# Cross terms of a complex product formed on VectorE instead of from copies made by ScalarE

## The chip, the cores and the metric

The kernel runs on one core of a Trainium2 chip. The metric is the device time of one execution in microseconds (us). In the tables and rows, PE is TensorE (PEld its weight loads), DVE is VectorE, ACT is ScalarE, POOL is GpSimd and SP is the queue that issues most DMAs. [...]

## The reference, cut to what matters

The output is a sum of the input, a long convolution per channel and a feed-forward network, both of the layer-normalized input. L = 2048 rows, D = 576 channels, 128 states, FF = 4608.

```
xn  = layernorm(x)
K   = Re sum_n C[d,n] exp(dt A[d,n] l) dt B[d,n]         # a kernel of 2048 taps per channel
y   = irfft(rfft(pad(xn)) * rfft(pad(K)))[:L] + xn*Dskip
out = x + y + silu(xn @ w1) @ w2
```

The product of the two spectra is a complex multiplication, element by element: with U = ur + i ui and K = kr + i ki, its real part is ur kr - ui ki and its imaginary part is ui kr + ur ki. The terms with ki are called cross terms here. They are what the change is about.

## The kernel before, in words

TensorE works through the feed-forward network from end to end: 18 chunks (`blocks`, two halves of the sequence times nine chunks of FF, each for two blocks of 512 rows), with matmuls called `ph` (x times w1, 128x512) and `po` (hidden times w2, 128x288). Each float32 operand is split into a high and a low part (`xh`, `xl`, `w1h`, `w1l`, `gh`, `gl`), and three partial products stand for one. For each `ph`, ACT applies silu (`gf`, L351) and rounds it (`gh`, L352) and DVE forms the low part (`gl`, L354); ACT also makes `w1h` and `w2h` and DVE `w1l` and `w2l` of each new weight; DVE adds each `po` to `acc` (L373).

The convolution is woven between these (`weave`): a generator `side` yields at marks of progress. Its stages are: normalization, the taps of the convolution kernel (`natural`, `kgen`, up to about 655 us), the spectral stage (`spectral`, about 655 to 975 us) and the last transform with the stores (`tail`).

The spectral stage handles 16 pairs of frequencies, p = 0 to 15. For each p it transforms a tile of the kernel (`kw`, kind 0), a tile of the input (`u`, kind 1) and, after the product, transforms back (`ysw`, kind 2). The matmuls (`pf`, L815) of all three are packed into 27 *visits* of TensorE, counted 0 to 26 here; a visit fills four PSUM banks, of which there is one set (`psb`, bufs=1), so that the next visit can start only when all copies out of the last have ended. ACT copies out `ka` and `ut` (L833) and `e` (L825); DVE forms the two halves of `yo` from `e` and PSUM (L827), `yo` is written to DRAM. Visit 5 holds the end of input 3, visit 16 the start of the back transform of product 8, visit 25 first the end of input 15 and then, as a second piece with feed-forward matmuls between, the back transform of product 14.

The *product* of p (`products`, L835 to L852) starts when its `ut` is complete. Real parts lie on partitions 0 to 63, imaginary parts on 64 to 127, and g counts two groups of 576 columns. ACT makes `kb` from `ka`, with the halves swapped and one negated (L840, L841), and then overwrites the imaginary half of `ka` by the real one (L842). DVE multiplies `kb` by the swapped `ut` (L845, L846), `ut` by `ka` (L847) and adds (L848). Four DMAs on SP (L851) then reorder the partitions into `ysw`, which a visit two or three places later reads. There is one `kb` for both groups, so ACT can't fill it for p+1 before the last addition of p. On DVE, the product is followed by `halves` (L799, L801), which prepares a later `kw`.

The order on each engine comes from a scheduler of the tile framework: it plays the program through with a cost model of its own and emits whatever it finds ready, by priority. If the instructions of one part change, others around it move too.

Of the kernel before, what the change touches and what calls it, by code (L numbers as in the profile page):

```python
# [11 lines left out]
F32 = mybir.dt.float32  # L12
# [3 lines left out]
ALU = mybir.AluOpType  # L16
# [3 lines left out]
P = 128  # L20
L = 2048
D = 576
# [21 lines left out]
def kernel(  # L44
# [22 lines left out]
    nc = tc.nc  # L67
# [22 lines left out]
    cst = ctx.enter_context(tc.tile_pool(name="cst", bufs=1))  # L90
    ident = cst.tile([P, P], F32, name="ident")
    f1 = vt = None
    s4 = None
# [16 lines left out]
    pss = psb = ps3 = None  # L110
# [39 lines left out]
    pins = {}  # L150
# [306 lines left out]
                    for kt in {"d3": (0, 1), "u1": (2, 3), "u2": (4,)}.get(step, ()):  # L457
                        split_xt(b, kt)

    kl = yp = pa = tail_at = None  # L460
    kf = {}

    def steps():

        NT, NP = 6, 96
        dt = cst.tile([NP, NT], F32, name="dt")
        nc.sync.dma_start(dt, log_dt.rearrange("(p t) -> p t", t=NT))

        e1 = cst.tile([NP, NT], F32, name="e1")
        e2 = cst.tile([NP, NT], F32, name="e2")  # L470
        ec = float(np.float32(math.e))
        nc.vector.memset(e1, ec)
        with behind(pins["xt7"]):
            nc.vector.tensor_scalar(e2, dt, 1.0 - math.log(ec), 1.0, op0=ALU.mult, op1=ALU.add)
        with behind(pins["sd"]):
            nc.gpsimd.tensor_tensor(e1, e1, dt, op=ALU.pow)
        nc.vector.tensor_mul(dt, e1, e2)
        dh = cst.tile([NP, NT], F32, name="dh")
        nc.vector.tensor_scalar(dh, dt, 0.5, None, op0=ALU.mult)
        return dt, dh  # L480

# [272 lines left out]
    def spectral():  # L754

        NP = 16
# [78 lines left out]
        def products(p):  # L835

            ut, ka = uts.pop(p), kas.pop(p)
            kb = kl.tile([P, 2, D], F32, tag="kb", name="kb", bufs=1)
            for g in range(2):
                nc.scalar.mul(kb[:64, g], ka[64:, g], -1.0)  # L840
                nc.scalar.copy(kb[64:, g], ka[64:, g])  # L841
                nc.scalar.copy(ka[64:, g], ka[:64, g])  # L842
            yield
            for g in range(2):
                nc.vector.tensor_mul(kb[:64, g], ut[64:, g], kb[:64, g])  # L845
                nc.vector.tensor_mul(kb[64:, g], ut[:64, g], kb[64:, g])  # L846
                nc.vector.tensor_mul(ut[:, g], ut[:, g], ka[:, g])  # L847
                pins["turned"] = nc.vector.tensor_add(ut[:, g], ut[:, g], kb[:, g]).ins  # L848
            ys[p] = kl.tile([P, 2, D], F32, tag="ys", name="ysw")
            for o in (0, 2, 1, 3):  # L850
                nc.sync.dma_start(ys[p][32 * o:32 * o + 32], ut[32 * (0, 2, 1, 3)[o]:32 * (0, 2, 1, 3)[o] + 32])  # L851
            yield  # L852
# [117 lines left out]
        return t + min(max(t - turn, 0) * lost / (0.5 - turn - lost), lost)  # L970

    def side():
        nonlocal s4, kl, yp, pa, tail_at, f1, vt, pss, psb, ps3
        marks = (0.13, 0.601, 0.876)
        tail_at = (0.91, 0.934, 0.967, 0.0072)
        with tc.tile_pool(name="kf", bufs=1) as kfp, tc.tile_pool(name="pss", bufs=3, space=PSUM) as pss, tc.tile_pool(name="ps3", bufs=1, space=PSUM) as ps3:
            for n in ("f", "phi"):
                kf[n] = kfp.tile([P, D], F32, name=n + "T")
            f1 = kfp.tile([P, P], F32, name="f1")
            vt = kfp.tile([P, 69], F32, name="vt")  # L980
            with tc.tile_pool(name="par", bufs=1) as par:
                with tc.tile_pool(name="pa", bufs=4) as pa:

                    zero = pa.tile([P, 512], BF16, name="zero", bufs=1)
                    nc.vector.memset(zero, 0.0)
                    pz = ps1.tile([P, 512], F32, tag="ps1", name="pz")

                    def idle(n):
                        for _ in range(n):
                            nc.tensor.matmul(pz, zero[:, :P], zero, start=True, stop=True)  # L990

                    idle(12)
                    p01, p23 = phase0(pa, (0, 1), idle), phase0(pa, (2, 3))
                    next(p01)
                    yield 0
                    next(p23)
                    yield 0
# [12 lines left out]
                    yield 0  # L1010
                with tc.tile_pool(name="nat", bufs=1) as nat, tc.tile_pool(name="pb", bufs=1) as pb:
                    nt = natural(nat, par)
                    def late(j):

                        xs = load_x(j, pb, "xj", (nc.sync,))
                        yield
                        with behind(pins["xn" if j == 8 else "gl"]):
                            normed(pb, (j, j + 1), xs)
                        yield

                    tiles = chain.from_iterable(late(j) for j in range(8, NJ, 2))
                    for at, todo in ((0.0, nt), (0.0, tiles), (0.004, tiles), (0.005, tiles), (gate_of(0), nt), (0.026, tiles), (0.028, tiles), (0.036, tiles), (0.038, tiles), (gate_of(1), nt), (0.06, tiles), (gate_of(2), nt), (0.09, nt)):
                        yield at
                        with behind(pins["gl"] if at else pins["xt7"] if todo is nt else None):
                            next(todo, None)
            with behind(pins["sd"]):
                nc.gpsimd.dma_start(f1, cf1)
            nc.sync.dma_start(vt, cv)
            with tc.tile_pool(name="up", bufs=1) as up:
                sp = spread(up)  # L1030
                for n, at in enumerate(kgen()):
                    yield paced(at, marks)
                    for off in (0.4, 0.8):
                        if n > 1 and n % 2 == (1 if off < 1 else 0):
                            yield paced(at + off % 1 / 36, marks)
                            next(sp, None)
                for _ in sp:
                    pass
        s4p = ctx.enter_context(tc.tile_pool(name="s4p", bufs=1))
        s4 = s4p.tile([P, 2, 32], F32, name="s4")  # L1040
        nc.gpsimd.dma_start(s4, cs4)

        ps3 = None
# [106 lines left out]
```

## Time and profile before

| what | us |
|---|---|
| median of 3 runs (lowest, highest) | 1095.03 (1094.64, 1095.66) |
| the profiled execution | 1095.03 |
| its span on the core | 1093.2 |
| PE busy | 1082.7 |
| DVE busy | 891.6 |
| ACT busy | 631.4 |
| POOL busy | 138.4 |

The span runs from the first to the last instruction of the program; 1.8 us of the execution lie around it. An interval in which TensorE is busy is not all spent at its peak, since the records of successive matmuls overlap. A row of the list of groups gives a line, the engine, the operation, tiles, shape and count, then the time the group kept its engine busy, the mean duration of one in ns, and the idle time just before them with what ended it. A row of the timeline gives start, duration and instruction, and in brackets the engine's idle time before it. A row of the windows gives a stretch, its length, the busy time of PE, PEld, DVE, ACT and POOL with their counts, the granted clock of TensorE (1.00 is full speed), the DMA share and GB/s.

### The profile page before, as it was taken

The numbers are of one execution on the slowest core, as the hardware profiler recorded it, in microseconds if no ns is written. First come the engines' busy times: TensorE is split into PE (matmuls) and PEld (weight loads), VectorE is DVE, ScalarE is ACT, GpSimd is POOL, SyncE is SP. The second block draws the span as 40 slices with busy tenths as digits, with TensorE's granted clock in tenths as the row PEclk, the third lists the DMA queues.
The fourth block names the chain that finished last, engine by engine and source line by source line (L and its number), as shares of the span: only waits on it lengthen the run. The fifth ranks groups of instructions, "written<-read, shape, count | busy, mean of one in ns | idle before, by whom it ended". The sixth has DMA issues, their size and how long they took to land.

```text
span 1093.2 us, 24683 instructions
## 1 busy us (share of the span) xinstructions
PE 1082.7 (99%) x10127; PEld 947.1 (87%) x10127; DVE 891.6 (82%) x1463; ACT 631.4 (58%) x998; POOL 138.4 (13%) x241
## 2 busy tenths in 40 slices
PE   9999999999999999999999999999999999999998
PEld 7999998998998999889999898878787787888886
DVE  7799899999999999999999954677987878553443
ACT  4574455767676777676676653746666665532210
POOL 1101000000000000010000004323242331000111
PEclk9999999999999999999999999999999999999999
DMA  9745521342525243427643257567676875337953
GB/s 263 215 125 157 141 68 40 94 112 66 130 71 134 71 110 95 112 89 193 211 132 102 73 113 189 147 180 221 196 218 175 232 195 160 101 101 205 244 161 87
DMA packets 175424, 156.58 MB, mean 143 GB/s; under 512 B 113312, under 2 KB 144800, under 8 KB 175184
## 3 DMA queue, kind: packets, MB, share of 16 engines
q1 hardware_dynamic: 159616, 103.21, 36.9%
q0 software_dynamic: 14944, 50.94, 15.5%
q8 instruction: 79, 1.29, 0.5%
q10 hardware_dynamic: 752, 0.85, 0.3%
q14 instruction: 33, 0.27, 0.1%
HBM read 101.00 MB, written 44.61 MB: 133 GB/s over the span
## 4 chain that ended last, share of the span: by engine, by line
PE 81%; DVE 10%; ACT 3%; DMA 3%; issue 2%; SPq 0%; POOL 0%; DVEq 0%; ACTq 0%
PE po L369 35%; PE ph L343 30%; PE pf L815 4%; PE ph L345 3%; PE ph L344 3%; PE kp L736 2%; PE z L663 1%; DVE acc L373 1%; PE py L950 1%; DMA acc<-in_A_u_dram 1%; DVE gl L354 1%; DVE th L649 1%; DMA ysw<-ut 1%; DVE w1l L305 1%; PE pu L171 1%
## 5 line engine op out<-in xcount | busy, mean ns | idle before, releaser
L369 PE MATMUL po<-w2h,gh 128*128 128x288 f32 x1152 | 338.8, 297 | 0.7 <-DVE acc L373 0.6
L369 PE MATMUL po<-w2l,gh 128*128 128x288 f32 x1152 | 338.5, 296 | 0.0
L369 PE MATMUL po<-w2h,gl 128*128 128x288 f32 x1152 | 336.0, 296 | 0.0
L369 PEld LDWEIGHTS po<-w2h,gh 128*128 128x128 f32 x1152 | 215.2, 188 | 15.2 <-issue 3.8
L369 PEld LDWEIGHTS po<-w2l,gh 128*128 128x128 f32 x1152 | 215.7, 188 | 8.4 <-issue 2.3
L369 PEld LDWEIGHTS po<-w2h,gl 128*128 128x128 f32 x1152 | 215.0, 188 | 5.3 <-issue 4.3
L351 ACT ACTIVATE gf<-ph 128x512 f32<-128x512 f32 (+1 forms) x146 | 85.7, 588 | 176.9 <-PE ph L345 157.6
L373 DVE TENSOR_TENSOR acc<-po,acc 128x288 f32<-128x288 f32 x288 | 126.7, 454 | 69.7 <-PE po L369 68.6
L343 PE MATMUL ph<-xh,w1l 128*128 128x512 f32 (+1 forms) x584 | 159.4, 387 | 0.0
L343 PE MATMUL ph<-xh,w1h 128*128 128x512 f32 (+1 forms) x584 | 158.9, 388 | 0.3 <-ACT w1h L303 0.3
L343 PE MATMUL ph<-xl,w1h 128*128 128x512 f32 (+1 forms) x584 | 158.3, 386 | 0.0
L354 DVE TENSOR_TENSOR gl<-gf,gh 128x512 fp32r<-128x512 f32 (+1 forms) x148 | 98.8, 673 | 44.6 <-ACT gh L352 43.6
L343 PEld LDWEIGHTS ph<-xh,w1l 128*128 128x128 f32 x584 | 106.9, 188 | 21.4 <-issue 1.4
L343 PEld LDWEIGHTS ph<-xl,w1h 128*128 128x128 f32 x584 | 107.2, 188 | 20.6
L343 PEld LDWEIGHTS ph<-xh,w1h 128*128 128x128 f32 x584 | 104.0, 188 | 17.4 <-ACT w1h L303 0.6
L352 ACT CAST gh<-gf 128x512 fp32r<-128x512 f32 (+1 forms) x148 | 89.1, 611 | 41.0 <-PE po L369 38.3
L174 POOL DMA_DIRECT2D d1u<-u x32 | 17.4, 543 | 478.8 <-ACT u L173 470.6
L693 ACT ACTIVATE c<-th,magic 128x1040 f32<-128x1040 f32 x36 | 42.0, 1167 | 39.7 <-DVE C L716 32.0
L695 ACT ACTIVATE c<-th 128x1040 f32<-128x1040 f32 x36 | 38.6, 1073 | 45.4 <-DVE th L694 45.3
L305 DVE TENSOR_TENSOR w1l<-w1r,w1h 128x640 fp32r<-128x640 f32 x72 | 57.0, 820 | 0.3 <-ACT w1h L303 0.3
L345 PE MATMUL ph<-x,w1l 128*128 128x512 f32 (+1 forms) x146 | 56.7, 389 | 0.0
L344 PE MATMUL ph<-x,w1h 128*128 128x512 f32 (+1 forms) x146 | 56.3, 386 | 0.0
(191 smaller groups left out, 1656.4 us busy)
## 6 DMA issues: line engine op xcount, KB each, us to landing
w2r<-in_B_w_dram SPq DMA_DIRECT2D x72, 288.0 KB, 3.7
w1r<-in_B_w_dram SPq DMA_DIRECT2D x35, 512.0 KB, 4.0
d1u<-u POOLq DMA_DIRECT2D x32, 288.0 KB, 2.8
d1k<-stage SPq DMA_DIRECT2D x36, 256.0 KB, 4.9
u<-d1u POOLq DMA_DIRECT2D x16, 576.0 KB, 5.3
kw<-d1k POOLq DMA_DIRECT2D x16, 576.0 KB, 5.2
ysw<-ut SPq DMA_DIRECT2D x64, 144.0 KB, 3.6
d<-yo POOLq DMA_DIRECT2D x32, 288.0 KB, 4.0
```

Of the source, the lines that this page charges most:

```text
L305: pins["w1l"] = nc.vector.tensor_sub(l1, src, h1).ins
L343: nc.tensor.matmul(ph, w[:, kt, :], v[:, kt, a:e], start=n + kt == 0, stop=False)
L344: nc.tensor.matmul(ph, h1[:, 4, :], x4[:, a:e], start=False, stop=False)
L345: pins["pe"] = nc.tensor.matmul(ph, l1[:, 4, :], x4[:, a:e], start=False, stop=True).ins
L351: nc.scalar.activation(gf, ph, AF.Silu)
L352: pins["gh"] = nc.scalar.copy(gh, gf).ins
L354: pins["gl"] = nc.vector.tensor_sub(gl, gf, gh).ins
L369: pins["pe"] = nc.tensor.matmul(po[:, :HD], G[blk, t][g][:, js], W2[half, c, t][w][:, hs], start=n == 0, stop=n == 3 * FT - 1).ins
L373: nc.vector.tensor_add(acc[j][:, hs], po[:, :HD], acc[j][:, hs])
L693: nc.scalar.activation(c65, th, AF.Identity, bias=magic)
L695: nc.scalar.activation(c65, th, AF.Abs)
L815: last = nc.tensor.matmul(banks[os, g, b, at:at + n], mats[p, kind // 2][gs, os], src[:, c:c + n], start=True, stop=True, tile_position=(6 ...
```

## The change

ACT's two copies into `kb` go. DVE forms the cross terms itself, from `ut` and the still unchanged imaginary half of `ka`: one as a plain multiplication, the other, with its sign, as a scalar_tensor_tensor with the constant -1.0. ACT's copy of the real half over the imaginary one (now L842 of the changed kernel) has to wait until both have read it, and DVE's next multiplication waits for that copy. `kb` is now one group large, with three buffers. All four steps of a product stand in one loop over g. To make room in SBUF, the small tiles of `steps` move to a pool that is released earlier, and the constant tables `f1` and `s4` no longer have tiles of their own: they are loaded over `ident`, so their DMAs on POOL have to wait until the last reader of what stood there before.

```
     def steps():
...
-        dt = cst.tile([NP, NT], F32, name="dt")
+        dt = kfp.tile([NP, NT], F32, name="dt")
...
         def products(p):
 
             ut, ka = uts.pop(p), kas.pop(p)
-            kb = kl.tile([P, 2, D], F32, tag="kb", name="kb", bufs=1)
             for g in range(2):
-                nc.scalar.mul(kb[:64, g], ka[64:, g], -1.0)
-                nc.scalar.copy(kb[64:, g], ka[64:, g])
+                kb = kl.tile([P, D], F32, tag="kb", name="kb", bufs=3)
+                nc.vector.tensor_mul(kb[64:], ut[:64, g], ka[64:, g])
+                nc.vector.scalar_tensor_tensor(kb[:64], ut[64:, g], -1.0, ka[64:, g], op0=ALU.mult, op1=ALU.mult)
                 nc.scalar.copy(ka[64:, g], ka[:64, g])
+                nc.vector.tensor_mul(ut[:, g], ut[:, g], ka[:, g])
+                pins["turned"] = nc.vector.tensor_add(ut[:, g], ut[:, g], kb).ins
             yield
-            for g in range(2):
-                nc.vector.tensor_mul(kb[:64, g], ut[64:, g], kb[:64, g])
-                nc.vector.tensor_mul(kb[64:, g], ut[:64, g], kb[64:, g])
-                nc.vector.tensor_mul(ut[:, g], ut[:, g], ka[:, g])
-                pins["turned"] = nc.vector.tensor_add(ut[:, g], ut[:, g], kb[:, g]).ins
             ys[p] = kl.tile([P, 2, D], F32, tag="ys", name="ysw")
...
-            f1 = kfp.tile([P, P], F32, name="f1")
+            f1 = ident
...
-        s4p = ctx.enter_context(tc.tile_pool(name="s4p", bufs=1))
-        s4 = s4p.tile([P, 2, 32], F32, name="s4")
+        s4 = ident[:, :64].rearrange("p (q k) -> p q k", q=2)
         nc.gpsimd.dma_start(s4, cs4)
```

The scheduler emits the same instructions as before on PE, in another order from the gap between visits 4 and 5 on; up to there the order on all engines but for the two loads is the same. ACT has 64 instructions fewer, DVE as many as before. Three places show what moves. In these rows a line number is that of the kernel the row is from.

On ACT between visits 7 and 9, before: the copies for product 5 (L840, L841) stand ahead of the rounding of two new weights (`w1h`, L303).

```order
L352 CAST gh<-gf 128x512
L840 ACTIVATE kb<-ka 64x576
L841 COPY kb<-ka 64x576
L840 ACTIVATE kb<-ka 64x576
L841 COPY kb<-ka 64x576
L303 CAST w1h<-w1r 128x640 x2
L326 CAST w2h<-w2r 128x576
L351 ACTIVATE gf<-ph 128x512
L842 COPY ka<-ka 64x576
L825 COPY e<-pf 128x448
```

The same place with the change:

```order
L842 COPY ka<-ka 64x576 x2
L352 CAST gh<-gf 128x512 x2
L351 ACTIVATE gf<-ph 128x512 x2
L352 CAST gh<-gf 128x512
L303 CAST w1h<-w1r 128x640 x2
L326 CAST w2h<-w2r 128x576
L352 CAST gh<-gf 128x512
L825 COPY e<-pf 128x448
```

No `kb` copy stands between `gh` and `w1h` any more; the two copies L842 of product 4 come ahead of all of it.

On ACT after visit 21, before: `e` of 128 columns and `e` of 448 columns are copies out of this visit, `ut` of 64 columns is the last of them.

```order
L825 COPY e<-pf 128x128
L840 ACTIVATE kb<-ka 64x576
L841 COPY kb<-ka 64x576
L840 ACTIVATE kb<-ka 64x576
L841 COPY kb<-ka 64x576
L842 COPY ka<-ka 64x576
L825 COPY e<-pf 128x448
L842 COPY ka<-ka 64x576
L351 ACTIVATE gf<-ph 128x512
L352 CAST gh<-gf 128x512
L833 COPY ut<-pf 128x2x64
```

With the change:

```order
L833 COPY ka<-pf 128x2x384
L825 COPY e<-pf 128x128
L825 COPY e<-pf 128x448
L351 ACTIVATE gf<-ph 128x512 x2
L833 COPY ut<-pf 128x2x64
```

Six of the eight instructions between the first `e` and `ut` that don't copy out of the visit are gone from between them.

On DVE, product 14, before: `gl` and two `w1l` of the feed-forward stand inside the product.

```order
L845 TENSOR_TENSOR kb<-ut,kb 64x576
L846 TENSOR_TENSOR kb<-ut,kb 64x576
L845 TENSOR_TENSOR kb<-ut,kb 64x576
L846 TENSOR_TENSOR kb<-ut,kb 64x576
L373 TENSOR_TENSOR acc_6374<-po,acc_6374 128x288
L827 TENSOR_TENSOR yo<-e,pf 128x256 x2
L847 TENSOR_TENSOR ut<-ut,ka 128x576 x2
L354 TENSOR_TENSOR gl<-gf,gh 128x512
L305 TENSOR_TENSOR w1l<-w1r,w1h 128x640
L848 TENSOR_TENSOR ut<-ut,kb 128x576
L305 TENSOR_TENSOR w1l<-w1r,w1h 128x640
L848 TENSOR_TENSOR ut<-ut,kb 128x576
```

With the change:

```order
L354 TENSOR_TENSOR gl<-gf,gh 128x512 x2
L305 TENSOR_TENSOR w1l<-w1r,w1h 128x640 x2
L840 TENSOR_TENSOR kb<-ut,ka 64x576
L373 TENSOR_TENSOR acc_6373<-po,acc_6373 128x288
L841 SCALAR_TENSOR_TENSOR kb<-ut,ka 64x576
L840 TENSOR_TENSOR kb<-ut,ka 64x576
L841 SCALAR_TENSOR_TENSOR kb<-ut,ka 64x576
L373 TENSOR_TENSOR acc_6373<-po,acc_6373 128x288
L827 TENSOR_TENSOR yo<-e,pf 128x256 x2
L843 TENSOR_TENSOR ut<-ut,ka 128x576 x2
L844 TENSOR_TENSOR ut<-ut,kb 128x576 x2
```

The feed-forward's instructions stand ahead of the product now. Product 8 moves alike: two `w1l` and a `w2l` that stood inside it come ahead of it.

On PE, the feed-forward matmuls that stand between two visits change in number. Where the prediction uses them, these are their counts, read from the order of both kernels:

| between | before | with the change |
|---|---|---|
| visits 4 and 5 | 21 po, 3 ph | 22 po, 3 ph |
| visits 5 and 6 | 26 po, 27 ph | 27 po, 18 ph |
| visits 6 and 7 | 38 po, 15 ph | 33 po, 12 ph |
| visits 14 and 16, both gaps | 56 po, 38 ph | 56 po, 33 ph |
| visits 21 and 22 | 33 po, 24 ph | 42 po, 30 ph |
| visits 24 and 25 | 30 po, 22 ph | 33 po, 22 ph |
| the two pieces of visit 25 | 22 po, 11 ph | 19 po |

More of the change, by code (lines that the diff above doesn't have):

```diff
@@ L458, in ffn @@
                         split_xt(b, kt)
-    kl = yp = pa = tail_at = None
+    kl = kfp = yp = pa = tail_at = None
     kf = {}
@@ L465, in steps @@
         NT, NP = 6, 96
-        dt = cst.tile([NP, NT], F32, name="dt")
+        dt = kfp.tile([NP, NT], F32, name="dt")
         nc.sync.dma_start(dt, log_dt.rearrange("(p t) -> p t", t=NT))
-        e1 = cst.tile([NP, NT], F32, name="e1")
-        e2 = cst.tile([NP, NT], F32, name="e2")
+        e1 = kfp.tile([NP, NT], F32, name="e1")
+        e2 = kfp.tile([NP, NT], F32, name="e2")
         ec = float(np.float32(math.e))
@@ L477, in steps @@
         nc.vector.tensor_mul(dt, e1, e2)
-        dh = cst.tile([NP, NT], F32, name="dh")
+        dh = kfp.tile([NP, NT], F32, name="dh")
         nc.vector.tensor_scalar(dh, dt, 0.5, None, op0=ALU.mult)
@@ L972, in side @@
     def side():
-        nonlocal s4, kl, yp, pa, tail_at, f1, vt, pss, psb, ps3
+        nonlocal s4, kl, kfp, yp, pa, tail_at, f1, vt, pss, psb, ps3
         marks = (0.13, 0.601, 0.876)
```

## The prediction

> **What bounds the kernel now.** I read the page first, then the windows, the waits of TensorE, the groups, and last the timeline around each wait.
>
> ```profile
> span 1093.2 us, 24683 instructions
> PE 1082.7 (99%) x10127; PEld 947.1 (87%) x10127; DVE 891.6 (82%) x1463; ACT 631.4 (58%) x998; POOL 138.4 (13%) x241
> 100.00:600.00 500.00, 499.56 (x5004) 454.54 (x5003) 479.15 (x728) 330.34 (x499) 22.17 (x38) 1.00 0.41 109
> 655.00:955.00 300.00, 297.39 (x2915) 243.43 (x2914) 223.32 (x372) 175.64 (x298) 89.24 (x155) 1.00 0.67 184
> ```
>
> TensorE is the bound: 1082.7 of 1093.2 us, at the full granted clock of 1.00. The change adds and removes nothing on TensorE. In the spectral stage, which it touches (second window), TensorE is idle for 300 - 297.4 = 2.6 us; that is what a better order of the other engines can win there. ACT, which loses work, is busy 176 of 300 us, so its load is no bound; only its order can matter. Who made TensorE wait in this stage is in the waits (us in total, times, longest):
>
> ```profile
> PE pf L815 <- ACT ut L833: 1.0, 1, 1.0
> PE pf L815 <- DMA ysw<-ut: 0.6, 1, 0.6
> PE pf L815 <- issue: 0.5, 1, 0.5
> PE ph L343 <- ACT w1h L303: 0.3, 1, 0.3
> ```
>
> Four waits, 2.5 us. The forecast is a ledger: which of the four go, and which new ones come where visits move closer to what feeds them.
>
> **The change, part by part.** First the work itself.
>
> ```profile
> L840 ACT ACTIVATE kb<-ka 64x576 f32<-64x576 f32 x32 | 21.9, 684 | 28.9 <-DVE ut L848 28.4
> L841 ACT COPY kb<-ka 64x576 f32<-64x576 f32 x32 | 21.5, 671 | 0.4
> L842 ACT COPY ka<-ka 64x576 f32<-64x576 f32 x32 | 20.9, 672 | 0.6
> L846 DVE TENSOR_TENSOR kb<-ut,kb 64x576 f32<-64x576 f32 x32 | 24.2, 756 | 1.0
> L847 DVE TENSOR_TENSOR ut<-ut,ka 128x576 f32<-128x576 f32 x32 | 23.5, 752 | 0.1
> L554 DVE SCALAR_TENSOR_TENSOR e<-ex,r 128x576 f32<-128x576 f32 x4 | 3.0, 750 | 0.0
> L801 DVE SCALAR_TENSOR_TENSOR kw<-kw,cwt 128x576 f32<-128x576 f32 x32 | 26.2, 817 | 0.7
> ```
>
> ACT loses 32 x 684 + 32 x 671 ns = 43.4 us, and the 28.4 us that it stood at the head of `kb`, waiting for the product before. DVE replaces 32 multiplications of 756 ns by 32 scalar_tensor_tensor. Their size has no row; the nearest is L554, also with a constant, 750 ns, so I take no difference. With the 817 ns of L801, whose scalar is a tile, it would be 32 x 61 ns = 2.0 us in 300 us, of which DVE is idle 77. Nothing of this is on TensorE's path by itself: cost 0, covered by the feed-forward matmuls.
>
> To turn rows of the order into time I need the pace of the matmuls, from the chain of waits:
>
> ```profile
> 1066.15 2.74 PE ph L343 x12
> 1069.35 4.78 PE po L369 x36
> ```
>
> One ph is 2.74/12 = 0.228 us, one po 4.78/36 = 0.133 us.
>
> *Wait for w1h (after visit 8).* Start, duration, idle time in brackets:
>
> ```profile
> 771.89 0.68 ACT L840 ACTIVATE kb<-ka 64x576 f32<-64x576 f32 x1
> 773.99 0.67 ACT L841 COPY kb<-ka 64x576 f32<-64x576 f32 x1
> 774.68 1.36 ACT L303 CAST w1h<-w1r 128x640 fp32r<-128x640 f32 x2
> 775.46 1.20 PE L343 MATMUL ph<-xh,w1h 128*128 128x512 f32 x4 [0.33 <-ACT w1h L303]
> ```
>
> Four kb copies, 2.8 us, run right ahead of the rounding for which TensorE waits. They are gone, so the wait goes: -0.33 (between -0.33 and 0, if the two gf ahead of it now come late).
>
> *Wait of visit 22 for visit 21's copies.*
>
> ```profile
> 907.28 0.69 ACT L840 ACTIVATE kb<-ka 64x576 f32<-64x576 f32 x1 [3.56 <-DVE ut L848]
> 910.77 0.53 ACT L825 COPY e<-pf 128x448 f32<-128x448 f32 x1
> 911.34 1.15 DVE L827 TENSOR_TENSOR yo<-e,pf 128x448 f32<-128x448 f32 x2 [0.16 <-ACT e L825]
> 913.18 0.26 ACT L833 COPY ut<-pf 128x128 f32<-128x128 f32 x1
> 913.49 1.09 PE L815 MATMUL pf<-kw,m 64*32 64x512 f32 x16 [1.04 <-ACT ut L833]
> ```
>
> kb copies, then e, then ut, the last copy out. Without them e and ut come earlier; besides, 9 po and 6 ph more stand between the visits, 2.6 us more room. The wait goes: -1.04 (to 0).
>
> *Waits for ysw (visits 16 and 25).* The product's end starts four DMAs; a visit reads what they land.
>
> ```profile
> 853.15 1.30 PE L815 MATMUL pf<-ysw,m 64*32 64x192 f32 x29 [0.62 <-DMA ysw<-ut]
> 937.48 0.75 DVE L845 TENSOR_TENSOR kb<-ut,kb 64x576 f32<-64x576 f32 x1
> 945.73 0.76 DVE L848 TENSOR_TENSOR ut<-ut,kb 128x576 f32<-128x576 f32 x1
> 946.96 2.78 SPq L851 DMA_DIRECT2D ysw<-ut  x4
> DMA to landing us min/median/max: 2.4/3.6/7.8
> 952.38 0.96 PE L815 MATMUL pf<-ysw,m 64*32 64x128 f32 x28
> ```
>
> Product 8, for visit 16: room shrinks by 5 ph, 1.1 us, but two w1l and a w2l, some 2.1 us when pipelined, leave the product for the place ahead of it. Arrival gains 1.0 on need: -0.62 (up to +1.1 if the product starts later by what now precedes it).
>
> Product 14, for the second piece of visit 25, was just in time: last issue at about 949.2, landing 3.6 later at 952.8, the piece at 952.38 (the first quarters land earlier). It runs 937.48 to 946.49. A gl and two w1l leave it (2.1 us), an acc enters (0.4): ready 1.7 us sooner. But 22 po + 11 ph (5.4 us) between the pieces become 19 po (2.5), 2.9 less, and 3 po (0.4) more ahead of the first: needed 2.5 sooner. New wait +0.8 (0 if DVE starts the product sooner; +3.5 if the two gl and two w1l that now stand ahead, 2.7 us, delay it in full).
>
> *Visits 5 and 7.*
>
> ```profile
> 736.52 1.27 DVE L827 TENSOR_TENSOR yo<-e,pf 128x512 f32<-128x512 f32 x2
> 738.09 0.88 PE L815 MATMUL pf<-kw,m 64*32 64x384 f32 x16 [0.52 <-issue]
> 759.65 0.59 ACT L833 COPY ut<-pf 128x512 f32<-128x512 f32 x1
> 760.64 1.20 PE L815 MATMUL pf<-kw,m 64*32 64x192 f32 x32
> ```
>
> Visit 5 comes 0.5 us late, right behind DVE's last yo of visit 4 (end 737.79); on DVE the same work stands ahead of that yo: 0 (one po more is -0.13; all of it would be -0.52). Visit 7 follows visit 6's last copy out (760.24) by 0.4. It is needed 9 ph less 1 po, then 5 po and 3 ph sooner: 3.3 us. ACT's four kb copies (2.7) are out of the way, which leaves a wait of 0.2; DVE's share of that chain isn't shorter, which gives up to 1.2. I take +0.4, nearer the ACT end, because the last copy was ACT's.
>
> *The handover.* L842 now waits for DVE and DVE for it. With both groups' cross terms ahead, the second copy (672 ns) runs beside the first multiplication (752): 0; behind other ACT work, up to 0.7 us per product, off TensorE's path while a visit has that to spare.
>
> *Tables in place of ident.*
>
> ```profile
> 132.31 0.55 POOL L158 DMA_DIRECT2D s<-in_cs_dram  x1 [24.75 <-ACT phiT L503]
> L663 PE MATMUL z<-f,kt x288: 272/272/373, 194.8 to 652.2; 64*128 64x128 f32 x144
> ```
>
> The load of f1 on POOL now waits for the last transposes, as the next entry of that queue, the load of s1, already did until 132; f1 is first read at 194.8. s4 waited for the same z matmuls before. 0. The ysw DMAs on SP now stand ahead of some weight loads, which are fetched a chunk ahead: 0.
>
> Sum: -0.33 - 1.04 - 0.62 + 0.8 + 0.4 = -0.79. The profiled execution took 1095.03, the median of the runs: 1094.2.
>
> [...] TensorE's weight loads are busy 90.9% of the first window (454.54/500), 81.1% of the second. [...]
>
> ```profile
> 655.00:955.00 300.00, 52.54 (x1488) 24.75 (x1488) 1.00 0.67 184
> ```
>
> These are the spectral matmuls alone (PE, PEld): small tiles whose loads are short. Without them the share is (243.43 - 24.75)/(300 - 52.54) = 88.4%, 2.5 points below the first window, 6 us. [...]
>
> **The rivals.**
> - *All waits go, none comes* (chance 0.27): also visit 5's, and the products start early enough for visits 7 and 25: -0.33 - 1.04 - 0.62 - 0.52 = -2.5, 1092.5. For it: ACT's 43 us and 28 us of blocked queue. Against: DVE has as much to do as before and is the later partner in visits 5 and 25.
> - *Products start later* (0.27): what left the products now delays their start. With s us of delay, visits 16 and 25 both lose s, so the sum is -0.79 + 2s: no gain from 0.4, over +2.2 from 1.5. In full (2.1 at visit 16, 2.7 at 25, 1.2 at visit 7): -0.33 - 1.04 + 1.1 + 3.5 + 1.2 = +4.4, 1099.5. For it: DVE needs weights and gh from ACT at that place. Against: ACT is freer.
> - *ACT is held as before* (0.10): L842's wait for DVE takes the place of the 28.4 us at L840, and the first two terms stay: -0.62 + 1.2 = +0.6, 1095.6.
> [...]
>
> **How the numbers follow.** The forecast has the rest, 0.34, and a range of its own of 1093 to 1095.6. 0.2%, 2.2 us, is about what a measurement of this kernel can tell from no change. Faster: the first and last rival, 0.29. Slower: the second, 0.27. Same: forecast and third, 0.44. The range goes to 1091.8 below (the first rival, whose waits can give a little more than their idle rows) and to 1098.8 above, most of the second.
>
> **What the profile after would show.** Right: no wait of TensorE for w1h or ut in this stage, visit 16 without idle time, the second piece of visit 25 waiting 0.5 to 1 us for ysw; L841 at about 0.75 us; L842 without long idle time before it. Wrong: TensorE waiting for ysw at several visits, or 28 us of ACT idle at L842. The forecast fails if the scheduler's new order meets waits that the old one never showed, since visits 5 to 25 all moved.

## The result and the profile after

The change makes the kernel a little faster: a median of 1091.95 us (1091.28 to 1092.68, 12 runs) against 1095.47 (1094.03 to 1096.55, 12 runs) for the kernel before, a ratio of 0.9969 with a 95% interval of 0.9961 to 0.9977. That is 3.4 us, by the ratio. The profiled execution took 1091.44 us, 3.59 less than that of the kernel before.

From the page of the changed kernel, and from its windows (columns as before: the stretch, its length, then busy time and count of PE, PEld, DVE, ACT and POOL, the granted clock, the DMA share, GB/s):

```profile
span 1089.7 us, 24623 instructions
PE 1080.4 (99%) x10127; PEld 946.9 (87%) x10127; DVE 892.1 (82%) x1463; ACT 588.7 (54%) x934; POOL 138.4 (13%) x241
100.00:600.00 500.00, 499.71 (x5005) 454.87 (x5004) 479.30 (x729) 330.68 (x499) 21.93 (x38) 1.00 0.41 109
655.00:955.00 300.00, 299.28 (x2926) 245.66 (x2925) 225.67 (x375) 133.16 (x237) 90.67 (x157) 1.00 0.67 185
```

ACT has lost 42.7 us, as its two kinds of copies took. DVE and POOL work as long as before, and TensorE has the same 10127 matmuls. In the spectral stage its idle time fell from 2.6 to 0.7 us. Who made it wait there (total, times, longest):

```profile
PE pf L815 <- issue: 0.4, 1, 0.4
PE po L369 <- DVE w2l L328: 0.3, 1, 0.3
```

Of the four waits of before, those for `ut` (1.0 us), `ysw` (0.6) and `w1h` (0.3) are gone. Visit 5's wait is still there, and a short one for `w2l`, at 740.2 us, is new. The groups of the product, from 655 to 985 us:

```profile
L840 DVE TENSOR_TENSOR kb<-ut,ka 64x576 f32<-64x576 f32 x32 | 24.2, 756 | 21.5 <-ACT ut L833 20.9
L841 DVE SCALAR_TENSOR_TENSOR kb<-ut,ka 64x576 f32<-64x576 f32 x32 | 24.1, 754 | 1.1
L843 DVE TENSOR_TENSOR ut<-ut,ka 128x576 f32<-128x576 f32 x32 | 23.4, 753 | 0.2
L842 ACT COPY ka<-ka 64x576 f32<-64x576 f32 x32 | 21.4, 672 | 23.4 <-DVE kb L841 23.3
```

The scalar_tensor_tensor takes 754 ns, as long as the multiplication (756) that it replaces. DVE waits 0.2 us in all for ACT's copy of the real half. And ACT is blocked again: for 23.4 us at L842, where before it was blocked for 28.9 us at L840. In the changed kernel that costs TensorE nothing that a row shows.

A comparison by place, from the timeline of TensorE. Visit 0 begins at 681.47 us instead of 682.27, 0.80 sooner, ahead of all that was changed in the order of the products. The last visit begins at 969.38 instead of 972.59, 3.21 sooner, though one `po` and one `ph` that stood behind it before now stand ahead of it (0.36 us by the pace of the matmuls). Counted like for like, the stage itself gave 3.21 - 0.80 + 0.36 = 2.8 us, and what follows it nothing.

At the places shown above, the orders that were read from the two kernels are the ones that the traces show, on ACT, on DVE and for the matmuls of TensorE. Only its weight loads (PEld) run ahead of matmuls: two or more of them start between two matmuls 728 times in 10127 in the trace of the changed kernel.

### The profile page after: what moved, and what is told of

It is laid out like the page before. It is cut to its first block, busy times and chain, and to the rows that moved or that the text cites. A ratio compares the mean times of both kernels' runs of the same rounds, so it can differ in the third digit from the quotient of the medians.

```text
span 1089.7 us, 24623 instructions
## 1 busy us (share of the span) xinstructions
PE 1080.4 (99%) x10127; PEld 946.9 (87%) x10127; DVE 892.1 (82%) x1463; ACT 588.7 (54%) x934; POOL 138.4 (13%) x241
## 4 chain that ended last, share of the span: by engine, by line
PE 90%; DVE 7%; ACT 1%; issue 1%; DMA 0%; POOL 0%; ACTq 0%; DVEq 0%
PE po L369 40%; PE ph L343 33%; PE pf L815 4%; PE ph L345 3%; PE kp L736 3%; PE ph L344 3%; PE z L663 2%; PE py L947 1%; DVE acc L373 1%; PE pu L171 1%; PE pu L172 1%; DVE gl L354 1%; DVE th L649 1%; DVE S L715 0%; DVE C L704 0%
```

## The experiments

All were compared with the kernel before on the same chip, whose median was 1095.0 to 1095.4 us each time. "Idle" in the table is what TensorE lacks of 330 us in the windows from 655 to 985 us, in the profiled execution. It is 2.6 us for the kernel before (327.39 busy) and 0.7 for the changed one (329.28 busy).

| kernel | median, us | ratio to before, 95% | idle, us |
|---|---|---|---|
| mem: the moves in SBUF alone | 1095.06 | 0.9991 to 1.0009 | 3.4 |
| act3: ACT's copies stay, kb by group, three buffers | 1094.28 | 0.9980 to 0.9997 | 1.4 |
| cross2: cross terms on DVE, two buffers, no moves | 1092.28 | 0.9959 to 0.9982 | 1.0 |
| extra: the change, with 43 us of ACT copies put back | 1091.86 | 0.9957 to 0.9979 | 0.4 |
| one: the change with one kb buffer | 1105.18 | 1.0077 to 1.0105 | 4.2 |
| oneyo: one, with two buffers for yo | 1095.88 | 0.9999 to 1.0017 | 3.8 |
| nocopy: the change, without ACT's last copy | 1108.47 | 1.0104 to 1.0135 | 5.3 |
| late: halves written ahead of the products | 1094.83 | 0.9987 to 1.0005 | 3.6 |
| due2: halves due a visit later | 1120.74 | 1.0212 to 1.0240 | 2.0 |
| e2: the change with two buffers for e | 1091.94 | 0.9958 to 0.9981 | 0.7 |
| split: ysw issued on two queues | 1091.31 | 0.9953 to 0.9978 | 0.7 |
| due4s: split, one chunk's halves a visit later | 1095.27 | 0.9995 to 1.0013 | 3.7 |

### Which part of the change carries it

**The moves in SBUF alone (mem).** `kb` and the product stay as before.

```
-        dt = cst.tile([NP, NT], F32, name="dt")
+        dt = kfp.tile([NP, NT], F32, name="dt")
...
-            f1 = kfp.tile([P, P], F32, name="f1")
+            f1 = ident
...
-        s4 = s4p.tile([P, 2, 32], F32, name="s4")
+        s4 = ident[:, :64].rearrange("p (q k) -> p q k", q=2)
```

> The moves in SBUF alone (dt, e1, e2, dh in the pool that is released early; f1 and s4 loaded over ident), products as before. Theory 1 (the gain comes from ACT's queue without the kb copies): no difference from before, within 0.5 us, and the four waits of TensorE in the spectral stage (w1h 0.33, ut 1.04, ysw 0.62, issue 0.52) as before. Theory 2 (the 0.6 us at the start and the 0.3 us in the tail, which the profile after is ahead outside the spectral stage, come from where tiles lie): 0.9 to 1.1 us faster than before.

The ratio is 1.0000 within 0.09%, and TensorE's waits in the stage are those of before:

```profile
PE pf L815 <- DMA ysw<-ut: 1.5, 1, 1.5
PE pf L815 <- ACT ut L833: 1.0, 1, 1.0
PE pf L815 <- issue: 0.4, 1, 0.4
PE ph L343 <- ACT w1h L303: 0.3, 1, 0.3
```

Two things follow. The 0.80 us that the changed kernel is ahead at visit 0 can't be counted as its gain: here visit 0 begins at 681.46 too, and the kernel isn't measurably faster. In the profiled executions of all kernels here, whose order is the same up to there, it begins anywhere from 681.2 to 682.5. And the wait for `ysw` at visit 16 is 1.5 us here and 0.6 in the profile of before, with the visits in the same places: it depends on when a transfer lands.

**The cross terms alone, with two buffers (cross2).** Only `products` is changed.

```
-                nc.scalar.mul(kb[:64, g], ka[64:, g], -1.0)
-                nc.scalar.copy(kb[64:, g], ka[64:, g])
+                nc.vector.tensor_mul(kb[64:], ut[:64, g], ka[64:, g])
+                nc.vector.scalar_tensor_tensor(kb[:64], ut[64:, g], -1.0, ka[64:, g], op0=ALU.mult, op1=ALU.mult)
```

> The cross terms on VectorE alone: products as changed, kb one group large with two buffers (the size of before's one), nothing moved in SBUF. Theory 1: 2.4 to 3.5 us faster than before, no wait of TensorE for w1h or ut in the spectral stage. Rival (the third buffer or the moved tiles carry it): 0 to 1.5 us faster, with DVE or ACT waiting for kb.

1092.28 us, and its interval contains that of the change. The trace shows every engine's instructions in the same order as in the changed kernel, but for where the two tables are loaded. So the cross terms carry the gain, with the order that they bring, and neither the third buffer nor the room made for it is needed. The waits are those of the changed kernel and one of 0.3 us for `ysw` at visit 16, which the changed kernel, in the same order, doesn't show: that visit's wait is gone by little.

**ACT's copies kept, but unblocked (act3).** `kb` per group with three buffers, filled by ACT as before.

```
-            kb = kl.tile([P, 2, D], F32, tag="kb", name="kb", bufs=1)
             for g in range(2):
+                kb = kl.tile([P, D], F32, tag="kb", name="kb", bufs=3)
+                kbs.append(kb)
...
-                nc.vector.tensor_mul(kb[:64, g], ut[64:, g], kb[:64, g])
+                nc.vector.tensor_mul(kb[:64], ut[64:, g], kb[:64])
```

> ACT makes the kb copies as before, but into one kb per group with three buffers, with the moves in SBUF: its head of the queue is blocked less, its 43 us of work stay. Theory 1 (the work stands in the way where it stands): at most 1 us faster, waits of TensorE for ACT (w1h, ut) of some 1 us stay in sum. Rival (what cost was ACT blocked for 28.4 us at L840 by the one buffer): about 2.5 us faster, ACT's idle time at L840 under 10 us.

1094.28 us, 1.1 below before by the medians: a third of the gain. ACT still waits for DVE at the first copy of a product, but less than half as long:

```profile
L842 ACT ACTIVATE kb<-ka 64x576 f32<-64x576 f32 x32 | 21.9, 684 | 12.3 <-DVE ut L850 11.6
...
PE po L369 <- DVE w2l L328: 0.6, 1, 0.6
PE pf L815 <- issue: 0.4, 1, 0.4
PE pf L815 <- DMA ysw<-ut: 0.3, 1, 0.3
```

The waits for `ut` and `w1h` are gone here too, with all of ACT's 43 us of copies still there.

**ACT's work put back (extra).** The change with two buffers for `kb`, and ahead of each product the four half copies into a tile that nobody reads.

```
             ut, ka = uts.pop(p), kas.pop(p)
+            junk = kl.tile([P, D], F32, tag="junk", name="junk", bufs=1)
+            for g in range(2):
+                nc.scalar.mul(junk[:64], ka[64:, g], -1.0)
+                nc.scalar.copy(junk[64:], ka[64:, g])
```

> The change with two buffers for kb, and with the four half copies of each product put back on ACT, into a tile that nobody reads (43 us of ACT work more, nothing else waits for it). Theory 1 (ACT's copies stood ahead of work that TensorE waits for): waits for ut or w1h come back, and the second copy of the real half starts up to 0.4 us later, so the visits that read a product just as it lands (7, 16, 25) lose up to 0.4 us each: 1 to 2.5 us slower than the change. Theory 2 (only the shorter way through DVE counts): within 0.5 us of the change, 1092.

1091.86 us: the whole gain, with ACT as busy as before. Only the smallest of the old waits came back:

```profile
PE ph L343 <- ACT w1h L303: 0.3, 1, 0.3
...
655.00:985.00 330.00, 329.61 (x3132) 271.27 (x3131) 240.10 (x401) 184.73 (x316) 92.63 (x161) 1.00 0.63 175
```

So the gain doesn't need ACT's shorter work. What the saved time is worth by itself this run doesn't tell, beyond the 0.3 us of `w1h`, because the scheduler's order is another here: between visits 4 and 5, for example, stand 28 `po` and 25 `ph` where the change has 22 and 3. The second theory's number came true, but not by its reason. From the end of the last copy of `ut` to the last addition, a product takes 7.7 us on the mean of 16 before, 7.4 in the change and 7.9 here (worked out from the timeline): it isn't a shorter way through DVE either. What this kernel and the change have in common is not one order either, only that in both orders hardly a visit stands where its data come late (0.4 and 0.7 us of idle time).

### What it takes to lose the gain

**One buffer for kb (one), and then two for yo (oneyo).**

```
-                kb = kl.tile([P, D], F32, tag="kb", name="kb", bufs=3)
+                kb = kl.tile([P, D], F32, tag="kb", name="kb", bufs=1)
```

And for the second kernel, beside it:

```
-                        yos[p] = kl.tile([P, 2, D], F32, tag="yo", name="yo", bufs=1)
+                        yos[p] = kl.tile([P, 2, D], F32, tag="yo", name="yo", bufs=2)
```

> The change with one buffer for kb instead of three: the cross terms of the second group wait for the first group's sum, which waits for ACT's copy. Theory 1 (the end of a product sets visits 7, 16 and 25): a product ends up to two handovers, 1.4 us, later, and those three visits wait up to 1.4 us each for ysw: 1 to 4 us slower than the change. Theory 2 (other work of DVE fills the handover): within 0.5 us of the change.

1105.18 us, 13 above the change, where 4 were expected at most. In the stage it shows what was expected, DVE waiting 11.7 us for ACT's copies and TensorE 3.6 us for `ysw`, at visits 16 and 21. The rest is at its end, in the timeline and the windows of this kernel:

```profile
986.63 1.20 POOL L854 DMA_DIRECT2D d<-yo  x2 [24.50 <-DVE yo L827]
991.38 0.35 DVE L827 TENSOR_TENSOR yo<-e,pf 128x64 f32<-128x64 f32 x2 [5.04 <-DMA d<-yo]
991.82 0.59 ACT L825 COPY e<-pf 128x512 f32<-128x512 f32 x1 [5.18 <-DVE yo L827]
992.43 1.28 DVE L827 TENSOR_TENSOR yo<-e,pf 128x512 f32<-128x512 f32 x2 [0.71 <-ACT e L825]
993.86 0.58 PE L369 MATMUL po<-w2h,gh 128*128 128x288 f32 x1 [3.78 <-DVE yo L827]
...
985.00:990.00 5.00, 5.00 (x25) 3.98 (x23) 1.15 (x2) 0.36 (x2) 1.20 (x2) 1.00 0.42 94
990.00:995.00 5.00, 1.22 (x6) 1.17 (x6) 1.64 (x4) 0.59 (x1) 0.99 (x2) 0.74 0.08 24
995.00:1000.00 5.00, 4.45 (x19) 4.10 (x19) 0.46 (x1) 0.00 (x0) 0.22 (x1) 0.50 0.51 118
1000.00:1005.00 5.00, 4.45 (x18) 3.92 (x17) 1.43 (x3) 2.68 (x5) 0.00 (x0) 0.50 0.79 250
```

The last `yo` of the stage goes where the `yo` before it still has to be written out, so DVE waits 5.0 us for that transfer. TensorE can go on with feed-forward matmuls meanwhile, but here they run out 3.8 us too soon: the last visit begins at 982.56, 13.2 us later than in the change, while TensorE's idle time before it is only 3.5 us longer. Some 8 us of feed-forward work (33 `po`, 16 `ph`) have moved ahead of it, and the clock cost another 1.7 (an estimate from the windows): it is 0.97, 0.50 and 0.96 in three windows of 3 us from 853 us, around and behind a wait of 2.63 us at visit 16. At the end the granted clock (third number from the end) is 0.50 for some 12 us of work. In the changed kernel the same `yo` waits for the same transfer, and TensorE has enough left to work on:

```profile
978.20 0.35 DVE L827 TENSOR_TENSOR yo<-e,pf 128x64 f32<-128x64 f32 x2 [3.38 <-DMA d<-yo]
```

> The kernel with one kb buffer (1105.2 us) with two buffers for yo. There the last yo of the stage waits 5 us for the transfer out of the yo before it, TensorE stands 3.8 us for that yo, and then its granted clock is 0.5 for 12 us. Theory 1 (that stall and the clock behind it are 3.8 + some 6 us of the 13): the stall goes, the clock stays at 1.0, 1095 to 1097. Theory 2 (the products' later ends cost the 13 us, and the end of the stage only shows it): 1102 or more.

1095.88 us: 9.3 us of the 13 came from that one wait and the clock behind it. The traces of both kernels show one order up to 964 us, so this comparison is a clean one. In the same windows TensorE now works on at full clock:

```profile
985.00:990.00 5.00, 5.00 (x27) 4.31 (x26) 2.67 (x6) 0.80 (x2) 2.19 (x4) 1.00 0.48 108
990.00:995.00 5.00, 3.90 (x28) 3.44 (x27) 0.92 (x2) 0.11 (x1) 0.21 (x1) 1.00 0.44 129
995.00:1000.00 5.00, 4.94 (x30) 4.20 (x30) 4.46 (x8) 5.00 (x10) 0.00 (x0) 1.00 0.90 281
```

What is left, 3.9 us above the change, is the stage: 3.3 us of waits for `ysw` and 0.5 for `ut`, and in the profiled execution 1.7 us of lower clock (0.58 and 0.86 in two windows of 3 us) behind the longest of them (2.46 us). That execution took 1097.32 us, the longest of ten, so the sum doesn't have to meet the median.

**The real half taken straight too (nocopy).** ACT makes no copy at all; DVE multiplies by the real half twice, 32 instructions of 0.75 us more.

```
-                nc.scalar.copy(ka[64:, g], ka[:64, g])
-                nc.vector.tensor_mul(ut[:, g], ut[:, g], ka[:, g])
+                nc.vector.tensor_mul(ut[64:, g], ut[64:, g], ka[:64, g])
+                nc.vector.tensor_mul(ut[:64, g], ut[:64, g], ka[:64, g])
```

> The change, and the products with the real half also taken straight from ka: two multiplications of 64 rows in place of one of 128, and no copy by ACT. DVE has 32 instructions of 0.75 us more (24 us of the 74 us that it is idle in the spectral stage), the handover to ACT and back is gone. Theory 1 (DVE is the late partner left): 1 to 3 us slower than the change, visit 5's wait 1.5 us longer. Rival (the 22 us that ACT waits for DVE at the copy of the real half is what is left to win): 0.5 to 1 us faster than the change.

1108.47 us, 16.5 above the change. In the stage TensorE waits 2.4 us for `acc`, 1.0 for `ysw`, 0.7 for `ut`; at its end is the same wait as in the kernel with one `kb`, and the same low clock behind it:

```profile
997.73 0.37 PE L369 MATMUL po<-w2h,gh 128*128 128x288 f32 x1 [4.61 <-DVE yo L827]
...
1000.00:1005.00 5.00, 3.90 (x16) 3.20 (x15) 0.92 (x2) 0.00 (x0) 0.00 (x0) 0.51 0.46 114
```

That wait and the clock behind it (0.81 and 0.51 in two windows of 5 us, so some 3.4 us lost) make 8 of the 16.5 us, and the longer waits in the stage 4.6; the rest isn't accounted for. How much of it is DVE's 24 us of added work, and how much the new order, no run separates, and whether two buffers for `yo` would cure this kernel too wasn't tried. One row of it answers a question of the prediction: visit 22 waits for `ut` although ACT has no copy of `ka` left at all. Only 30 `po` and 15 `ph` stand ahead of that visit here, 42 and 30 in the change.

```profile
922.68 1.09 PE L815 MATMUL pf<-kw,m 64*32 64x512 f32 x16 [0.72 <-ACT ut L833]
```

**Halves ahead of the products (late).**

```
+            for p in due.get(v, ()):
+                with behind(pins["turned"]) if "turned" in pins else nullcontext():
+                    halves(p)
             for kind, p in ends[v]:
                 if kind == 1:
                     for _ in products(p):
                         pass
-            for p in due.get(v, ()):
-                with behind(pins["turned"]):
-                    halves(p)
```

> The change with the halves of a later chunk (three instructions of 0.82 us on DVE) written ahead of the products of a visit instead of behind them. The rival of the prediction in which products start later, made on purpose: two or three halves, 1.6 to 2.5 us, between a product's steps. Theory 1 (three visits read their product as it lands): waits for ysw of 1.6 to 2.5 us at each of visits 7, 16 and 25, 4 to 7 us slower than the change, more than the 2s that the prediction took for two visits. Theory 2 (the products have room): at most 1 us slower.

1094.83 us, 2.9 above the change: nothing is left of the gain. The places weren't those expected. Visit 2 waits 1.99 us for `ysw` and visit 16 0.46, a `ph` waits 1.0 us for `w1h`; visits 7 and 25 show no wait. And in the profiled execution the wait of 2 us cost more than itself, since the granted clock fell behind it:

```profile
705.58 0.67 PE L815 MATMUL pf<-ysw,m 64*32 64x192 f32 x16 [1.99 <-DMA ysw<-ut]
...
703.00:706.00 3.00, 1.01 (x40) 0.43 (x24) 2.65 (x5) 2.25 (x4) 2.47 (x5) 1.00 0.91 201
706.00:709.00 3.00, 3.00 (x25) 2.83 (x14) 2.32 (x4) 2.40 (x5) 1.49 (x3) 0.61 0.99 323
709.00:712.00 3.00, 3.00 (x18) 2.83 (x17) 2.93 (x7) 0.84 (x2) 0.00 (x0) 0.82 1.06 357
```

Of these 6 us, 3 x 0.39 + 3 x 0.18 = 1.7 were lost to the clock. This execution took 1097.06 us, the longest of eleven. Its mean granted clock is 0.998, and three others of 0.997 and 0.998 took 1096.4; the seven of 0.999 and 1.000 took 1093.9 to 1095.0. So the median, 1094.83, doesn't hold the loss by the clock.

**Halves due later (due2, due4s).** In the changed kernel DVE works without a gap up to the `yo` that visit 5 waits for, and three halves stand ahead of it:

```profile
732.50 0.76 DVE L844 TENSOR_TENSOR ut<-ut,kb 128x576 f32<-128x576 f32 x1
733.17 0.81 DVE L799 SCALAR_TENSOR_TENSOR kw<-kw,cwt 128x576 f32<-128x576 f32 x1
734.02 1.67 DVE L801 SCALAR_TENSOR_TENSOR kw<-kw,cwt 128x576 f32<-128x576 f32 x2
735.61 0.45 DVE L373 TENSOR_TENSOR acc<-po,acc 128x288 f32<-128x288 f32 x1
735.98 1.28 DVE L827 TENSOR_TENSOR yo<-e,pf 128x512 f32<-128x512 f32 x2
...
737.36 0.88 PE L815 MATMUL pf<-kw,m 64*32 64x384 f32 x16 [0.45 <-issue]
```

```
-            due.setdefault(min(span[0, p - 2][1] + 1, span[0, p][0] - 1), []).append(p)
+            due.setdefault(min(span[0, p - 2][1] + 2, span[0, p][0] - 1), []).append(p)
```

> The change with the halves of most later chunks due one visit later. In the change DVE works without a gap from 726.6 to 737.9 us (a product, three halves of 2.5 us, acc, the last yo of visit 4), and visit 5 starts 0.1 us after that yo. Theory 1 (DVE's queue in front of yo sets visit 5): with the halves behind it the wait of 0.4 us goes, and so may the wait for w2l; 0.4 to 0.7 us faster than the change. Theory 2: the halves, now closer to the visit that reads them, and whatever they are put ahead of make new waits: as late as the change or slower.

1120.74 us, the slowest of all. Visit 5's wait is gone (an `acc` of 0.9 us is waited for just ahead of it), and the stage runs with 2.0 us of idle time, no more than before. But all feed-forward matmuls of the stage now stand ahead of the last visits, and the end lies bare: TensorE waits 13.8 us for the last `ysw` and 9.3 for the last `yo`, and the granted clock is 0.50 in each window of 5 us from 990 to 1020 us.

```profile
PE pf L815 <- DMA ysw<-ut: 13.8, 1, 13.8
PE po L369 <- DVE yo L827: 9.3, 1, 9.3
...
1015.00:1020.00 5.00, 4.45 (x18) 4.10 (x19) 0.46 (x1) 0.59 (x2) 0.00 (x0) 0.50 0.52 140
```

Then one chunk alone, on top of the kernel with two queues (below):

```
-            due.setdefault(min(span[0, p - 2][1] + 1, span[0, p][0] - 1), []).append(p)
+            due.setdefault(min(span[0, p - 2][1] + 1 + (p == 4), span[0, p][0] - 1), []).append(p)
```

> The kernel with ysw issued on two queues (1091.3 us), and with the halves of one chunk alone, chunk 4, due a visit later, so that they stand behind the yo for which visit 5 waits; 452 + 71 feed-forward matmuls are left after the last visit, as there. Theory 1 (DVE's queue in front of that yo sets visit 5): the wait of 0.4 us goes and no other comes, 1090.6 to 1091.0. Theory 2 (moved halves make a new wait at the next visits, as in the run with most of them moved): 1091.5 or more.

Moving three instructions of one chunk, with the same matmuls left for the end of the stage, takes 4.0 us from the kernel with two queues (1091.31 to 1095.27): all of the gain. The `yo` of visit 4 does come 1.3 us sooner than in the change, at 734.65, but the scheduler puts 8 us more of feed-forward work ahead of visit 5, and later visits meet their data at other times:

```profile
PE po L369 <- DVE acc L373: 2.4, 3, 1.2
PE pf L815 <- issue: 1.2, 2, 0.9
```

### What no longer matters

**Two buffers for e (e2).** `kb` has two buffers here. Every engine's instructions stand in the same order as in the changed kernel.

```
-                    e = kl.tile([P, 512], F32, tag="e", name="e", bufs=1)[:, :n]
+                    e = kl.tile([P, 512], F32, tag="e", name="e", bufs=2)[:, :n]
```

> The change with two buffers for kb and two for e, every engine's instructions in the same order: only ACT's copy of e no longer waits for DVE's two yo of the piece before. Theory 1 (visit 5's wait of 0.4 us is the chain e, yo, e, yo of visit 4): the wait goes, ACT's idle time at e falls from some 4 us a time, and the time falls by 0.4 to 0.8 us. Theory 2 (that chain is set by DVE, not by the buffer): visit 5 still waits and the time is that of the change.

1091.94 us, no difference, and visit 5 still waits 0.4 us. It is DVE's queue, not the buffer.

**The reordering transfers on two queues (split).**

```
-            for o in (0, 2, 1, 3):
-                nc.sync.dma_start(ys[p][32 * o:32 * o + 32], ut[32 * (0, 2, 1, 3)[o]:32 * (0, 2, 1, 3)[o] + 32])
+            for i, o in enumerate((0, 2, 1, 3)):
+                (nc.sync, nc.gpsimd)[i % 2].dma_start(ys[p][32 * o:32 * o + 32], ut[32 * (0, 2, 1, 3)[o]:32 * (0, 2, 1, 3)[o] + 32])
```

> The change with two of the four DMAs of ysw issued on POOL's queue instead of all four on SP's (four issues take 2.45 us there). Theory 1 (visits 7, 16 and 25 read their product 0.2 us after it lands, so that they are just not held up any more): the products land up to 1.2 us sooner, and as there is no wait left to remove the time stays, within 0.3 us of the change. Theory 2 (those visits are still held up, in gaps too short for a row): up to 0.6 us faster. If POOL's own transfers stand ahead of them in the queue, ysw lands later and one of those visits shows a wait.

1091.31 us, 0.6 below the change, which the intervals don't tell apart. The products do land sooner: the last transfer of product 8, for visit 16, lands at 849.4 us instead of 852.2. But no wait of TensorE for `ysw` appears or goes. It is the fastest kernel measured here, and faster than before by more than its interval.

## Why the prediction was right, and where its steps failed

The time lies in the predicted range (1091.8 to 1098.8), 0.15 us above its lower end, which was taken from a rival and not from the forecast. It is 2.2 us below the forecast, and so on the side of faster, which had a chance of 0.29, by 0.31% where 0.2% was the bound to no change. The ledger was right on what goes and wrong on what comes. By its steps:

| step | predicted, us | measured, us |
|---|---|---|
| wait for `w1h` | -0.33 | -0.33 |
| visit 22's wait for `ut` | -1.04 | -1.04 |
| visit 16's wait for `ysw` | -0.62 | -0.62 |
| visit 5 | 0 | -0.07 (0.52 to 0.45) |
| visit 7, new | +0.4 | 0 |
| second piece of visit 25, new | +0.8 | 0 |
| wait for `w2l`, not foreseen | 0 | +0.27 |
| sum | -0.79 | -1.79 |

**The waits that go** were read rightly, each at its place. The reason given for two of them, ACT's copies standing ahead, is borne out for `w1h` (with ACT's work put back, ACT works without a gap from 766 to 776 us, and 0.3 us came back at the same place) but not for visit 22: its wait stays away with ACT's copies put back, and with them never removed, and it comes (0.72 us) in the kernel where ACT copies nothing of `ka`. What remains is the second reason that the step names, the new place of the visit: 42 `po` and 35 `ph` stand ahead of it in the first two of these kernels, 30 and 15 in the third. In the changed kernel itself `e` and `ut` hardly come earlier: with the `kb` copies gone ACT waits for DVE instead, and the last `ut` ends at 913.2 us where it ended at 913.4.

```profile
911.19 0.53 ACT L825 COPY e<-pf 128x448 f32<-128x448 f32 x1 [4.29 <-DVE yo L827]
```

At visit 16 the wait is gone by little: with the same order it was 0.3 us in cross2.

**The waits that come** were the steps that failed, and they hold most of the miss. For visit 25 the product was taken to be ready 1.7 us sooner and needed 2.5 sooner. In the changed kernel:

```profile
936.62 0.76 DVE L840 TENSOR_TENSOR kb<-ut,ka 64x576 f32<-64x576 f32 x1 [1.51 <-ACT ut L833]
942.63 1.42 DVE L844 TENSOR_TENSOR ut<-ut,kb 128x576 f32<-128x576 f32 x2
944.12 3.12 SPq L848 DMA_DIRECT2D ysw<-ut  x4
949.35 1.04 PE L815 MATMUL pf<-ysw,m 64*32 64x128 f32 x32
```

The product starts 0.9 us sooner (936.62 against 937.48): visit 24 comes 0.4 sooner, and an `acc` no longer stands ahead of it. It takes 7.4 instead of 9.0 us, and its last issue ends at 947.24 instead of some 949.7: 2.5 sooner. The transfers then land 2.4 to 3.0 us after their issue, not 3.4 to 3.7 as before, so the last one lands at 949.16 instead of 952.24, 3.1 sooner. The piece is needed 3.0 sooner, as its start shows, and has no wait. The step took off what leaves the product, but left its start where it was, and it kept the time to landing. That second term decides: with the 3.43 us that the last transfer took before, instead of 2.52, the last quarter would have landed at 950.07 and the piece would have waited some 0.7 us (an estimate from these times), nearly the +0.8 forecast. The shorter landing shows again in cross2 (2.6 to 3.1 us), in the same order; what makes it shorter isn't shown. The step also put the landing before at 952.8, after the start of the piece, where the trace has it at 952.24, 0.14 us ahead of it. Visit 7 fell by the same mistake: visit 6's last copy of `ut` ends at 756.64 instead of 760.24, 3.6 us sooner instead of the 2.7 that ACT's copies took, because visit 6 itself comes 2.1 sooner. A step that shifts what needs the data has to shift what feeds them along with it.

**The handover.** L842 was to show no long idle time, and 28 us there were to be a sign of failure. There are 23.4, and it is no failure: ACT waits there while TensorE waits for nothing of ACT's. The price for TensorE, 0, was right; idle time of ACT there was the wrong sign of failure to choose. The size of the scalar_tensor_tensor, 750 against 754 ns, was right.

**The rest.** The sum by rows accounts for 1.8 of the 3.4 us. TensorE's idle time in the stage fell by the same amount, 1.9 us. By the places of the visits the stage gave 2.8, so 0.9 lie where no row shows idle time; 0.3 of it is visit 16, which took 2.95 us from its first matmul to its last before and 2.06 in the changed kernel, 0.9 less where the row counts 0.62. The wait for `ysw` may be larger in most executions of the kernel before than in the profiled one. The kernel with the moves alone, where it is 1.5 us and visit 0 begins where it does in the change, suggests that: against it the stage gave 3.4 us by the same count, all of the gain. For the kernel before itself it isn't shown, and this part stays open.

**The rivals.** The first, all waits go and none comes, is nearest in time (1092.5), but by places it is half right: visit 5's wait stayed. "Products start later" did not come, and its price was tried: brought about by an edit, it took 2.9 us, though at visits 2 and 16 instead of 16 and 25 and in an order of its own. "ACT is held as before" came true as an event and cost nothing. The 0.29 for faster also holds 0.02 for room hidden behind TensorE's busy row, a term of 6 us that no run shows. What the runs showed there is the weight loads' share of the stage, 81.1% before and 81.9% in the changed kernel (245.66/300), up by about what the idle time lost.

What the prediction missed as a whole is how much hangs on the scheduler's order. Its last sentence, that the new order may meet waits that the old one never showed, was the right worry: three moved instructions of one chunk cost 4.0 us. Five kernels with the cross terms on DVE, at least two buffers and the halves in their place have the gain, and one such (nocopy) hasn't. Four of the five share one order, by their traces (split leaves it at 949 us); the fifth, extra, has another. So the gain stands on two orders, not on five. Why these are nearly free of waits, and whether that is more than luck, isn't settled.

## What to carry to other kernels

When TensorE is full, take no credit for time that another engine saves: 43 us of ACT work could be put back without any loss, in another order. Price such a change by the few places where TensorE really waits, shift both the need and its feeders there, and allow several us either way for the order, which a small edit can change. Look at the end of a stage as well: count the matmuls that are left to cover its last chain of copies and transfers, because a bare end cost more (9.3 us in one kernel, some 6 of them by the lower clock, an estimate from its windows) than all waits inside.

## What the runs showed of the hardware that was not expected

- Some waits of TensorE had a second price here, the granted clock behind them. Behind a wait of 1.55 us (visit 16 of the kernel with the moves alone) it stayed at 1.00; behind 1.99 us (halves ahead of the products) it fell to 0.61 and 0.82 in two windows over the next 6 us; behind 2.46 us (one `kb` buffer, two for `yo`) to 0.58 and 0.86 in two such windows; behind 3.78 us (one `kb` buffer) it was 0.50 for some 12 us, in which a `po` took 0.24 us instead of 0.133. How the clock follows from a wait isn't shown. The kernel without ACT's last copy lost some 3.4 us to the clock behind a wait of 4.61 us, the one with one `kb` buffer some 6 behind its 3.78 (both estimates from the windows), and of the eleven executions of the kernel with the halves ahead four have a mean granted clock of 0.997 or 0.998 and seven one of 0.999 or 1.000.
- A scalar_tensor_tensor of 64x576 with a constant takes 754 ns, as a plain multiplication does (756); with a tile as its scalar, 128x576 takes 817.
- Four transfers of one kind in the same place of the same order landed so that visit 16 waited 0.6 us in one profiled execution (before) and 1.5 in another (mem).
